# Folds split into halves and spread over a window's steps, row loads issued a window later

## The chip, the cores and the metric

The kernel runs on one NeuronCore of a Trainium2 chip. The metric is the device time of one launch in microseconds, taken as the median of several runs. PE (TensorE), DVE (VectorE), ACT (ScalarE) and POOL (GpSimd) each run their own instructions in the order in which the program lists them, and wait for one another by semaphores; SP (SyncE) and POOL issue the DMAs.

## What is computed

```python
def _attn_ref(x):                       # x: 8 x 3008 x 256
    X = np.fft.fft(x, axis=1)
    X = np.fft.fft(X, axis=2)
    return X.real.astype(np.float32)

def _moe_ref(x, w_in, w_out):           # x: 24064 x 256, w_in: 256 x 2048, w_out: 2048 x 256
    h = np.maximum(x @ w_in, 0.0)
    return (h * h @ w_out).astype(np.float32)
```

The real part of a two-dimensional Fourier transform mixes each of the 8 sequences over its 3008 positions and its 256 features. A feed-forward layer follows, with a squared relu between its two products. Inputs reach the kernel as float32 and are worked on in half precision on the chip; the output is float32.

## The kernel before

**Symmetry.** A real Fourier transform of row k and of row 3008 - k share their products. The kernel computes a cosine part `zc` and a sine part `zs` for half the rows only. A step's sum of both gives one half of the output rows, and turning the sign of the sine part gives the mirrored half. Before the matmuls each sequence is *folded*: rows are added to or subtracted from their mirror images, over features and positions, which shrinks what has to be multiplied.

**Units, blocks, windows.** The eight sequences are taken in the order i = 0 to 7 (`bs` puts sequence 0 last, so i = 7 is sequence 0, and i = 6 is the last sequence in memory, `b + 1 == B`). Each gives two units, odd rows (i, 0) and even rows (i, 1), laid behind one another as columns. The columns are cut into 25 windows, of 512 columns from window 6 on. A window w has eight steps s0 to s7 (`NST`). In each step PE does the first feed-forward product for 256 of the 2048 hidden features of this window (lines 804 to 831), and an eighth of the second product of the window before (`part`, L679). In between it computes z for units that a later window needs (`z_steps`, L567).

**Two kinds of steps.** In a plain step, `pq` (L808, L809) forms the sum, ACT takes its relu (L840), `turn` (L831) changes the sine's sign in PSUM, and ACT takes the relu of the mirrored half. A step listed in `diff[w]` goes another way: `cosines` (L817), then on DVE `twice` (L821) forms t = n - 2 cos, `sines` (L826) adds the sine part, ACT takes one relu and DVE the other (`TENSOR_ADD_SAT`, L838) with the help of t. The rows n are made on POOL: `spread_nyq` brings one row of `zs` to all partitions (PE, then ACT as `zn`, L761), and `nyq_rows` multiplies it (L769), two instructions a step, into three buffers of the pool `wp`. Where step 0 is in the next window's list, the first two of these stand at s5 and the others at s6 of the window before; else at s6 and s7. There are two PSUM buffers for the sums (`ps_h`), so step s + 2 can't start before both relus of step s are done. Squares are DVE's (`power`, L847), which `settle` lets run a step later, or ACT's (`power_act`, L851).

**Loading and folding a sequence.** `load_x` fills a tile of four quarters: two direct quarters and two whose rows come in reverse order by an indirect DMA (`gather`, L132). Two sequences need a row by itself. For sequence 7 (i = 6) the index of the third quarter differs (`idx_c`) and row 1 of that quarter comes by a small DMA (L150); for sequence 0 (i = 7) one row of the first quarter does (L143). Each of them overwrites what a gather has put there, and waits for that gather.

`fold_steps(i)` returns the jobs of one sequence, all but the DMAs on DVE:
- `d_even`: copy a row (L417), add features to their mirror into `fe` (L418, 3072 elements a partition), copy column 0 of all quarters (L419)
- `n_cos` (L429), `d_odd` (L422, 3072 elements), `n_sin` (L432), `odds` (L435, what the odd unit needs), `nyq` (two tiny PE matmuls and a copy, L440 to L442)
- `even` (L447), and in the same job the store of its result to `scr` in DRAM (L449); `back` reads it from there in another order (L457, L459), for the even unit
- `late`: `fold8(0)`, `fold8(1)` (L473), `fold16(0)`, and `fold16(1)` (L484) with `nyq8` (L490 to L492, four copies)
- `load`: `load_x` of the next sequence

**Where the jobs stand.** For i from 2 on, a list is written out by hand: `at_of[w][s]` holds the jobs run in step s of window w behind that step's first relu, `post_of` those behind its share of the second product. With b0 = 5, 8, 10, 13, 16, 19 for i = 2 to 7, `d_even` stands in window b0 - 1 at s1 (at s5 for i = 2 and i = 4), `n_cos` two steps behind it, `d_odd` at s0 of b0, `n_sin` and `odds` at s1, `even` at s3, `nyq` behind s3, `back` at s6, `load` at s7; the late folds in b0 + 1 at s3, s3, s5, s7. For i = 4 window b0 - 1 = 9 is also that of the late folds of i = 3. The order in these lists is the order of each engine's queue.

## Time and profile before

| | |
|---|---|
| median of 3 runs | 631.01 us (630.08 to 633.45) |
| the profiled execution | 630.0 us, span of its instructions 628.0 us |
| mean granted TensorE clock | 0.994 |
| PE busy | 592.7 us (94%) |
| DVE busy | 484.2 us (77%) |
| ACT busy | 460.7 us (73%) |
| POOL busy | 338.9 us (54%) |
| DMA | 47.50 MB, mean 76 GB/s |

A line of the timeline view reads: start and length in us, engine, line of the kernel, operation, what is written and read, how many instructions are merged, and in brackets the idle time of the engine before it with what ended it. A line of the waits view reads: the waiting instruction, what released it, then us in total, times, and the longest. In the windows view the columns are the busy us of each engine, the granted clock, and DMA. "Idle" in brackets is counted from the end of the instruction before, which for PE is a modelled one.

### The profile page before, as it was taken

The numbers are of one execution on the slowest core, as the hardware profiler recorded it, in microseconds if no ns is written. First come the engines' busy times: TensorE is split into PE (matmuls) and PEld (weight loads), VectorE is DVE, ScalarE is ACT, GpSimd is POOL, SyncE is SP. The second block draws the span as 40 slices with busy tenths as digits, with TensorE's granted clock in tenths as the row PEclk, the third lists the DMA queues.
The fourth block names the chain that finished last, engine by engine and source line by source line (L and its number), as shares of the span: only waits on it lengthen the run. The fifth ranks groups of instructions, "written<-read, shape, count | busy, mean of one in ns | idle before, by whom it ended". The sixth has DMA issues, their size and how long they took to land.

```text
span 628.0 us, 11263 instructions
## 1 busy us (share of the span) xinstructions
PE 592.7 (94%) x4441; PEld 427.6 (68%) x4441; DVE 484.2 (77%) x607; ACT 460.7 (73%) x624; POOL 338.9 (54%) x248
## 2 busy tenths in 40 slices
PE   4889999999999999999899979999799999999997
PEld 2457786676666776776677746777467776777786
DVE  7787666978888679878887868878588788777760
ACT  6687777878777776877687856878468787787762
POOL 8220225268808617498086673865838558538520
PEclk9999999999999999999999989999899999999999
DMA  8945321124511461236113431132511311111112
GB/s 150 141 89 131 111 69 33 46 81 84 119 41 43 111 137 43 73 78 133 45 36 106 101 74 49 38 108 66 104 33 50 103 47 49 47 39 44 52 55 67
DMA packets 36523, 47.50 MB, mean 76 GB/s; under 512 B 4215, under 2 KB 30327, under 8 KB 36471
## 3 DMA queue, kind: packets, MB, share of 16 engines
q0 software_dynamic: 9344, 22.14, 17.7%
q1 hardware_dynamic: 26899, 24.44, 13.1%
q8 instruction: 34, 0.56, 0.4%
q10 hardware_dynamic: 228, 0.21, 0.1%
q14 instruction: 18, 0.15, 0.1%
HBM read 33.63 MB, written 27.84 MB: 98 GB/s over the span
## 4 chain that ended last, share of the span: by engine, by line
PE 65%; DVE 13%; POOL 9%; DMA 6%; issue 4%; ACT 3%; POOLq 0%; DVEq 0%
PE po L679 37%; PE ph L831 5%; PE ph L808 5%; PE ph L809 5%; POOL n L769 5%; PE ph L826 5%; PE ph L817 3%; PE pz L567 3%; DVE t L821 3%; DVE h L847 3%; DVE h L838 3%; ACT h L840 2%; DMA xo<-in_x_dram,idx_c 2%; DMA xo<-in_x_dram,idx_f 2%; DMA xo<-in_x_dram,idx_r 1%
## 5 line engine op out<-in xcount | busy, mean ns | idle before, releaser
L840 ACT ACTIVATE h<-ph 128x1024 f16<-128x1024 f32 (+3 forms) x311 | 295.6, 990 | 102.2 <-PE ph L826 82.7
L679 PE MATMUL po<-wout,h 128*128 128x256 f16 (+1 forms) x3024 | 362.8, 273 | 0.0
L769 POOL TENSOR_SCALAR n<-zn,g2n 128x512 f32<-128x512 f16 (+2 forms) x146 | 264.8, 1829 | 165.8 <-ACT zn L761 165.5
L679 PEld LDWEIGHTS <-h 128*128 128x128 f16 (+1 forms) x3024 | 297.2, 99 | 73.1 <-issue 1.3
L847 DVE TENSOR_TENSOR h<-h 128x1024 f16<-128x1024 f16 (+6 forms) x216 | 193.8, 908 | 33.4 <-ACT h L840 30.7
L838 DVE CUSTOM_DVE_ANT_0 h<-t,ph 128x1024 f16<-128x1024 f32 x67 | 81.8, 1221 | 47.7 <-ACT h L840 47.3
L821 DVE SCALAR_TENSOR_TENSOR t<-ph,n 128x1024 f32<-128x1024 f32 (+2 forms) x73 | 87.6, 1200 | 29.7 <-PE ph L817 22.3
L808 PE MATMUL ph<-zc,gh 128*128 128x512 f16 (+3 forms) x238 | 88.4, 372 | 0.4 <-ACT h L900 0.3
L809 PE MATMUL ph<-zs,gh 128*128 128x512 f16 (+3 forms) x238 | 88.4, 372 | 0.0
L851 ACT ACTIVATE h<-h 128x1024 f16<-128x1024 f16 (+2 forms) x73 | 76.1, 1043 | 0.0
L831 PE MATMUL ph<-zs,gh 128*128 128x512 f16 (+3 forms) x238 | 68.1, 368 | 0.0
L694 ACT ACTIVATE osb<-po 128x512 f32<-128x512 f32 (+3 forms) x95 | 55.2, 585 | 11.4 <-PE po L679 10.0
L826 PE MATMUL ph<-zs,gh 128*128 128x512 f16 (+2 forms) x146 | 43.6, 380 | 17.0 <-DVE t L821 16.9
L817 PE MATMUL ph<-zc,gh 128*128 128x512 f16 (+2 forms) x146 | 42.8, 375 | 0.0
L809 PEld LDWEIGHTS <-gh 128*128 128x128 f16 x238 | 23.4, 98 | 26.4 <-issue 1.9
L808 PEld LDWEIGHTS <-gh 128*128 128x128 f16 x238 | 23.4, 98 | 25.7 <-issue 1.1
L826 PEld LDWEIGHTS <-gh 128*128 128x128 f16 x146 | 13.8, 97 | 22.6 <-issue 19.4
L572 ACT ACTIVATE es<-pz 128x376 f32<-128x376 f32 (+1 forms) x32 | 15.5, 487 | 17.5 <-PE pz L567 17.4
L831 PEld LDWEIGHTS <-gh 128*128 128x128 f16 x238 | 22.1, 98 | 5.4
L817 PEld LDWEIGHTS <-gh 128*128 128x128 f16 x146 | 14.3, 98 | 16.7
L459 POOL DMA_INDIRECT rb<-scr,idx_r x16 | 20.6, 1288 | 4.9 <-issue 4.9
L132 POOL DMA_INDIRECT xo<-in_x_dram,idx_r x15 | 18.3, 1219 | 4.5 <-issue 4.0
(142 smaller groups left out, 355.3 us busy)
## 6 DMA issues: line engine op xcount, KB each, us to landing
out_dram<-osb SPq DMA_DIRECT2D x77, 128.0 KB
xo<-in_x_dram POOLq DMA_DIRECT2D x7, 768.0 KB
scr<-ev POOLq DMA_DIRECT2D x8, 390.0 KB, 2.8
rb<-scr POOLq DMA_DIRECT2D x16, 130.0 KB
out_dram<-osb SPq DMA_DIRECT2D x12, 94.0 KB
w<-in_moe_w_in_dram POOLq DMA_DIRECT2D x2, 512.0 KB, 11.2
wout<-in_moe_w_out_dram POOLq DMA_DIRECT2D x1, 1024.0 KB
out_dram<-osb SPq DMA_DIRECT2D x8, 75.0 KB
```

The lines of the kernel that those rows point to most:

```text
L679: nc.tensor.matmul(po[0:m, j * D : (j + 1) * D], h2[:, fc, q : q + m], wout16[:, fc, :], start=(fc == 0), stop=(fc == NFC - 1))
L769: nc.gpsimd.tensor_scalar(out=n2[:, a, 0:wn1], in0=zns[wt][:, 0:wn1], scalar1=g2n[:, fc : fc + 1], scalar2=None, op0=ALU.mult)
L808: nc.tensor.matmul(ph[:, a, 0:wn], gh[:, 0, f0 : f0 + P], zcw[:, 0:wn], start=True, stop=False)
L809: nc.tensor.matmul(ph[:, a, 0:wn], gh[:, 1, f0 : f0 + P], zsw[:, 0:wn], start=False, stop=True)
L817: nc.tensor.matmul(ph[:, a, 0:wn], gh[:, 0, f0 : f0 + P], zcw[:, 0:wn], start=True, stop=True)
L821: nc.vector.scalar_tensor_tensor(out=t2[:, :, 0:wn], in0=phs[s][:, :, 0:wn], scalar=-2.0, in1=n2s[w, s][:, :, 0:wn], op0=ALU.mult, op1=ALU ...
L826: nc.tensor.matmul(phs[s][:, a, 0:wn], gh[:, 1, f0 : f0 + P], zsw[:, 0:wn], start=False, stop=True, skip_group_check=True)
L831: nc.tensor.matmul(phs[s][:, a, 0:wn], gh[:, 2, f0 : f0 + P], zsw[:, 0:wn], start=False, stop=True, skip_group_check=True)
L838: nc.vector._custom_dve(TENSOR_ADD_SAT, out=h, in0=t2s[s][:, :, 0:wn], in1=phs[s][:, :, 0:wn], s0=BIG, s1=0.0)
L840: nc.scalar.activation(h, phs[s][:, :, 0:wn], AF.Relu, bias=0.0, scale=-1.0)
L847: nc.vector.tensor_tensor(h, h, h, op=ALU.mult)
L851: nc.scalar.activation(h, h, AF.Square, bias=0.0, scale=1.0)
```

## The change

Seven things change together.

1. `load_x` no longer issues the two small row loads. They move to `load_rows(i)`, which is put at s7 of window b0 - 2 of that sequence, a window after the gathers.
2. `d_even` and `d_odd` can do half of the quarters at a time (0 and 1, or 2 and 3). The first half of `d_even` also does both copies, for i > 1 on ACT.
3. `d_even`'s halves stand two steps apart (s1, s3; for i = 2 at s5, s7; for i = 4 at s5, s6), `n_cos` behind them (s5; s0 of b0 for i = 2; s7 for i = 4).
4. In b0 the halves of `d_odd` stand at s0 and s1, `n_sin` at s2, `odds` at s5 and `nyq` behind s6.
5. The store to `scr` becomes a job of its own, `away`, at s4.
6. `nyq8` does two copies in place of four, and is a job of its own; the five late jobs stand at s3 to s7 of b0 + 1.
7. `diff` of window 9 becomes (0, 2) in place of (2, 6), so the rows n for its s0 are made in window 8.

```diff
         gather(2, idx["r" if b + 1 < B else "c"][:, 0:1], o + (S - R * (P - 1)) * D)
+        gather(3, idx["r"][:, 0:1], o + (H - R * (P - 1)) * D)
+        return t
+
+    def load_rows(i):
+
+        b, t = bs[i], xs[i]
+        o = b * S * D
+        if b == 0:
+            nc.gpsimd.dma_start(out=t[0:1, 0, R - 1, :], in_=bass.AP(tensor=x.tensor, offset=x.offset + o, ap=[[D, 1], [1, D]]))
         if b + 1 == B:
             nc.gpsimd.dma_start(
                 out=t[1:2, 2, :, :].rearrange("p c d -> p (c d)"),
                 in_=bass.AP(tensor=x.tensor, offset=x.offset + o + (S - R) * D, ap=[[XW, 1], [1, XW]]))
-        gather(3, idx["r"][:, 0:1], o + (H - R * (P - 1)) * D)
-        return t
...
-        def d_even():
-            nc.vector.tensor_copy(t[0:1, 2, 0, :], t[0:1, 0, R - 1, :])
-            nc.vector.tensor_tensor(fef[:, :, 1:129], lo, hi, op=ALU.add)
-            nc.vector.tensor_copy(fef[:, :, 0:1], xf[:, :, 0:1])
-
-        def d_odd():
-            nc.vector.tensor_tensor(fof[:, :, 1:129], lo, hi, op=ALU.subtract)
+        def d_even(h=None):
+            a, z = (0, 4 * R) if h is None else (2 * R * h, 2 * R * (h + 1))
+            if a == 0:
+                for o, v in ((t[0:1, 2, 0, :], t[0:1, 0, R - 1, :]), (fef[:, :, 0:1], xf[:, :, 0:1])):
+                    if i > 1:
+                        nc.scalar.activation(o, v, AF.Copy, bias=0.0, scale=1.0)
+                    else:
+                        nc.vector.tensor_copy(o, v)
+            nc.vector.tensor_tensor(fef[:, a:z, 1:129], lo[:, a:z], hi[:, a:z], op=ALU.add)
+
+        def d_odd(h=None):
+            a, z = (0, 4 * R) if h is None else (2 * R * h, 2 * R * (h + 1))
+            nc.vector.tensor_tensor(fof[:, a:z, 1:129], lo[:, a:z], hi[:, a:z], op=ALU.subtract)
...
+
+        def away():
             scr = drp.tile([R * P, 260], F16, name="scr", tag="scr")
...
-            for slot in range(2):
-                nc.vector.tensor_copy(xt[:, 0, slot, :, 130:131], rev_dim(xt[:, 1, 1 - slot, :, 128:129], 1))
-            nc.vector.tensor_copy(spn[:, 0, :, 0:1], yt[:, 1, 0, :, 128:129])
-            nc.vector.tensor_copy(spn[:, 1, :, 0:1], yt[:, 0, 0, :, 128:129])
-
-        late = [lambda: fold8(0), lambda: fold8(1), lambda: fold16(0), lambda: (fold16(1), nyq8())]
+            nc.vector.tensor_copy(xt[:, 0, :, :, 130:131], rev_dim(rev_dim(xt[:, 1, :, :, 128:129], 1), 2))
+            nc.vector.tensor_copy(spn[:, :, :, 0:1], rev_dim(yt[:, :, 0, :, 128:129], 1))
+
+        late = [lambda: fold8(0), lambda: fold8(1), lambda: fold16(0), lambda: fold16(1), nyq8]
...
     for i in range(2, B):
         b0 = (win_of(col_of[i, 0]) + win_of(col_of[i - 1, 1])) // 2 - 1
-        both = i > 2 and len(at_of[b0 - 1][3]) > 0
-        at_of[b0 - 1][0 if i > 2 else 5].append(lambda i=i: make(i))
-        put(at_of, b0 - 1, 5 if i == 2 or both else 1, i, "d_even")
-        put(at_of, b0 - 1, 7 if i == 2 or both else 3, i, "n_cos")
-        for s, name in ((0, "d_odd"), (1, "n_sin"), (1, "odds"), (3, "even"), (6, "back"), (7, "load")):
-            put(at_of, b0, s, i, name)
-        put(post_of, b0, 3, i, "nyq")
+        tight = b0 - 2 in [(win_of(col_of[j, 0]) + win_of(col_of[j - 1, 1])) // 2 - 1 for j in range(2, i)]
+        near = i == 2 or tight
+        at_of[b0 - 1][0].append(lambda i=i: make(i))
+        at_of[b0 - 2][7].append(lambda i=i: load_rows(i))
+        put(b0 - 1, 5 if near else 1, i, "d_even", 0)
+        put(b0 - 1, (6 if tight else 7) if near else 3, i, "d_even", 1)
+        put(b0 if i == 2 else b0 - 1, 0 if i == 2 else 7 if near else 5, i, "n_cos")
+        put(b0, 0, i, "d_odd", 0)
+        put(b0, 1, i, "d_odd", 1)
+        put(b0, 2, i, "n_sin")
+        put(b0, 3, i, "even")
+        put(b0, 4, i, "away")
+        put(b0, 5, i, "odds")
+        put(b0, 6, i, "back")
+        put(b0, 6, i, "nyq", d=post_of)
+        put(b0, 7, i, "load")
+        for k, s in enumerate((3, 4, 5, 6, 7)):
+            late(b0 + 1, s, i, k)
         if b0 > 5:
             diff[b0] = (2, 4, 6)
-        for st in range(4):
-            at_of[b0 + 1][(3, 3, 5, 7)[st]].append(lambda i=i, st=st: folds[i]["late"][st]())
-        if both:
-            diff[b0 - 1] = (2, 6)
+        if tight:
+            diff[b0 - 1] = (0, 2)
```

The sequences i = 0 and i = 1, which windows 1 to 4 fold, keep whole folds and copies on DVE; only `away`, the order of the copies in `d_even` and the five late jobs reach them.

More of the change, by code (lines that the diff above doesn't have):

```diff
@@ L142, in load_x @@
             gather(0, idx["f"][:, 0:1], o + D)
-            nc.gpsimd.dma_start(out=t[0:1, 0, R - 1, :], in_=bass.AP(tensor=x.tensor, offset=x.offset + o, ap=[[D, 1], [1, D]]))
             direct(1, 2)
@@ L488, in nyq8 @@
             xt, yt = st["xt"], st["yt"]
-            for slot in range(2):
-                nc.vector.tensor_copy(xt[:, 0, slot, :, 130:131], rev_dim(xt[:, 1, 1 - slot, :, 128:129], 1))
-            nc.vector.tensor_copy(spn[:, 0, :, 0:1], yt[:, 1, 0, :, 128:129])
-            nc.vector.tensor_copy(spn[:, 1, :, 0:1], yt[:, 0, 0, :, 128:129])
-        late = [lambda: fold8(0), lambda: fold8(1), lambda: fold16(0), lambda: (fold16(1), nyq8())]
-        return {"u_odd": u_odd, "u_part": u_part, "v_even": v_even, "v_part": v_part, "d_even": d_even, "n_cos": n_cos, "odds": odds, "d_odd": d_odd, "load": load, "n_sin": n_sin, "nyq": nyq, "even": even, "back": back, "late": late}
+            nc.vector.tensor_copy(xt[:, 0, :, :, 130:131], rev_dim(rev_dim(xt[:, 1, :, :, 128:129], 1), 2))
+            nc.vector.tensor_copy(spn[:, :, :, 0:1], rev_dim(yt[:, :, 0, :, 128:129], 1))
+        late = [lambda: fold8(0), lambda: fold8(1), lambda: fold16(0), lambda: fold16(1), nyq8]
+        return {"u_odd": u_odd, "u_part": u_part, "v_even": v_even, "v_part": v_part, "d_even": d_even, "n_cos": n_cos, "odds": odds, "d_odd": d_odd, "load": load, "n_sin": n_sin, "nyq": nyq, "even": even, "away": away, "back": back, "late": late}
     gh = const.tile([P, 3, F], F16, name="gh")
@@ L714, in fold_jobs @@
         f = folds[i] = fold_steps(i)
-        return [f["d_even"], f["n_cos"], lambda: (f["d_odd"](), f["load"]()), f["n_sin"], f["odds"], f["nyq"], f["even"], f["back"]]
+        return [f["d_even"], f["n_cos"], lambda: (f["d_odd"](), f["load"]()), f["n_sin"], f["odds"], f["nyq"], lambda: (f["even"](), f["away"]()), f["back"]]
     NST = NFC // 2
@@ L720, with put, late @@
     diff = {w: (0, 2, 4, 6) if w > 5 else (4, 6) for w in range(4, NW)}
-    def put(d, w, s, i, name):
-        d[w][s].append(lambda: folds[i][name]())
+    def put(w, s, i, name, *k, d=at_of):
+        d[w][s].append(lambda: folds[i][name](*k))
+    def late(w, s, i, *st):
+        at_of[w][s].append(lambda: run(*[folds[i]["late"][k] for k in st]))
     def make(i):
@@ L784 @@
             te = table_steps(1)
-            at = [[folds[1]["even"]], [lambda: te["freq"](), lambda: te["args"](0)], [lambda: f0s["v_part"](0)], [lambda: f0s["v_part"](1), f0s["even"], f0s["back"]],
+            at = [[folds[1]["even"], folds[1]["away"]], [lambda: te["freq"](), lambda: te["args"](0)], [lambda: f0s["v_part"](0)], [lambda: f0s["v_part"](1), f0s["even"], f0s["away"], f0s["back"]],
                   [lambda: te["turns"](0)], [lambda: te["mods"](0)], [lambda: te["absm"](0), lambda: te["sins"](0)], [lambda: te["coss"](0)]]
@@ L788 @@
             at[0] = [lambda: te["weigh"]()]
-            for st in range(4):
-                at[1 + st // 2] = at[1 + st // 2] + f0s["late"][st : st + 1]
+            for st in range(5):
+                at[1 + st // 3] = at[1 + st // 3] + f0s["late"][st : st + 1]
             at[3] = [folds[1]["back"]]
@@ L793 @@
         elif w == win_of(col_of[1, 1]) - 1:
-            for st in range(4):
-                at[st] += folds[1]["late"][st : st + 1]
+            for st in range(5):
+                at[min(st, 3)] += folds[1]["late"][st : st + 1]
             lo, hi = 4, NST - 1
```

## The prediction

> **What bounds the kernel now.** First the page: TensorE is busy 94% of a span of 628.0 us, so only the time in which it stands still can be won. Then the table of waits, which names what it stands for:

> ```profile
> PE ph L826 <- DVE t L821: 16.9, 13, 4.5
> ...
> POOL xo L150 <- DMA xo<-in_x_dram,idx_c: 9.6, 1, 9.6
> ...
> POOL xo L143 <- DMA xo<-in_x_dram,idx_f: 8.9, 1, 8.9
> ...
> DVE t L821 <- POOL n L769: 7.1, 2, 4.1
> ```

> The columns are us in total, times, longest. Once the start is over, almost every stop of PE is one kind: `sines` (L826) waits for `twice` (L821) on DVE, 13 times. Twice that goes back to POOL, whose rows L769 stood behind two small loads that waited for a gather to land. I call windows w, their steps s0 to s7, and T the start of a window's first cosines. Window 15, POOL, then PE:

> ```profile
> 354.29 1.01 POOL L132 DMA_INDIRECT xo<-in_x_dram,idx_c  x1 [0.30 <-issue]
> 364.94 0.57 POOL L150 DMA_DIRECT2D xo<-in_x_dram  x1 [9.64 <-DMA xo<-in_x_dram,idx_c]
> ...
> 366.86 14.69 POOL L769 TENSOR_SCALAR n<-zn,g2n 128x512 f32<-128x512 f16 x8
> ```

> ```profile
> 365.61 1.91 PE L679 MATMUL po<-wout,h 128*128 128x256 f16 x16
> 371.32 1.01 PE L826 MATMUL ph<-zs,gh 128*128 128x512 f16 x2 [3.79 <-DVE t L821]
> 372.12 0.63 PE L808 MATMUL ph<-zc,gh 128*128 128x512 f16 x1
> 372.55 0.63 PE L809 MATMUL ph<-zs,gh 128*128 128x512 f16 x1
> ```

> Sixteen such matmuls start 1.75 apart in all, so L826 could have started at 367.36 and lost 3.96 (by starts; the bracket counts from a modelled end, some 0.17 less). Then matmuls start 0.43 apart where 0.22 is usual: the clock is halved for some 2.5 us (0.79 over 368 to 376), 1.26 more. Window 18 has 4.64 and 1.26 likewise (450.23).

> The other stops are big folds ahead of `twice` on DVE. Window 12 (T = 290.16):

> ```profile
> 290.84 0.42 DVE L484 TENSOR_TENSOR xy<-xy 128x520 f16<-128x520 f16 x1
> 291.18 0.65 DVE L490 COPY xy<-xy 128x2 f16<-128x2 f16 x2
> ...
> 291.88 1.21 DVE L821 SCALAR_TENSOR_TENSOR t<-ph,n 128x1024 f32<-128x1024 f32 x1
> ...
> 296.83 0.48 DVE L417 COPY xo<-xo 1x256 f16<-1x256 f16 x1
> 297.35 2.19 DVE L418 TENSOR_TENSOR fe<-xo 128x3072 f16<-128x3072 f16 x1
> 299.46 0.20 DVE L419 COPY fe<-xo 128x24 f16<-128x24 f16 x1
> 299.55 1.21 DVE L821 SCALAR_TENSOR_TENSOR t<-ph,n 128x1024 f32<-128x1024 f32 x1
> ```

> ```profile
> 297.05 1.91 PE L679 MATMUL po<-wout,h 128*128 128x256 f16 x16
> 300.81 0.59 PE L826 MATMUL ph<-zs,gh 128*128 128x512 f16 x2 [1.85 <-DVE t L821]
> ```

> Here 297.05 + 1.75 = 298.80 against 300.81: 2.0 lost. By the same reading the stops before L826 are: w4 1.24 (and 0.26 behind it), w6 0.24, w7 0.70 and 1.64, w8 0.71, w9 0.50, w10 0.81, w12 0.81 and 2.02, w15 3.96 and 0.49, w18 4.64 and 0.74, w21 0.81; with 2 x 1.26 of slow clock, 22.1 us. This is the pot.

> **The change, part by part.**

> *Last fold of s7 moved to s6, four nyquist copies made two.* At s7 DVE had fold16 and four copies (290.84 to 291.88, 1.04) ahead of `twice`. What stays is a copy of four columns and one of spn; single copies took 0.32 and 0.16, so some 0.4. Fold16 now stands in s6, where DVE waits 0.81 for ACT anyway. `twice` starts 0.65 earlier, and the stops at s0 (0.70, 0.81, 0.81 in w7, w12, w21) fall to 0.05, 0.15, 0.15. Gain 2.0; bounds 1.2 (copies as dear as before) to 2.3 (nothing left).

> *d_even in halves, its two copies on ACT.* The 297 to 299.55 stretch is 2.7 of DVE. Left at s1 is one half: 2.19 / 2 = 1.1, or 1.79 / 2 = 0.9 as the same fold took where POOL was idle (w9). So `twice` comes 1.6 earlier: w12 2.02 to 0.35, w7 1.64 to 0.05 (PE has z work until 172.8 there), w4 1.24 + 0.26 to 0.1. The second half meets `twice` of s4 with 1.1 where n_cos of 0.96 stood and lost 0.05: nothing. n_cos goes to s5. Gain 4.7; bounds 2.7 (each half 0.5 dearer, with 0.5 in each second place) and 5.2. The copies on ACT are not in the trace: 128x6 took 0.23 there (L400), 128x256 0.39; I take 0.35 and 0.25. ACT sat idle 3.38 before its next relu in w12, which covers them; uncovered they cost 0.6 in six windows, 3.6.

> [...]

> *d_odd in halves at s0 and s1, n_sin at s2, odds at s5, its nyquist step at s6.* Before, w8 had n_sin 0.96 and odds 1.26 between the power at 194.25 and `twice` at 197.66; now a half d_odd of 0.9 stands there. The stops of 0.71 and 0.81 (w8, w10) go; three of 0.13 in w13, w16, w19 also. At s5 odds of 1.2 is less than the 2.5 that d_even put there in w4. Its nyquist matmuls come at s6, a step after odds, so PE need not wait for them. Store at s4 in a job of its own: POOL's wait of 2.3 for DVE before it moves, and nobody waits for POOL there. Gain 1.9; bounds 1.2 and 2.0.

> *Late folds one a step* (w6 0.24 to 0.1): 0.15.

> *Window 9 (i = 4, tight).* d_even was at s5, 0.50 lost; diff (2, 6) becomes (0, 2), the same number. But the rows for its s0 are now due in w8 and stand in POOL's queue ahead of the four scr reads: two rows 3.4, reads 4.4, two rows 3.4, starting 4.8 before T (as in w12, 285.42 against 290.16). So x's load goes out at T + 6.5 instead of T + 1.9, and its last gather, which landed at 230.44 = T + 16.3, at T + 20.9. ACT meets its fe copy in s5 near T + 18.3 and stands 2.6; behind it are relu (1.0) and osb, and PE's s7 (T + 22.5) finds its PSUM at T + 23.1. I take 0.6: this window breaks even (-0.1). Bounds: 0 and 3 (a gather of 12 us as measured, and 2 more).

> *The small loads.* They leave the queue between the gathers: rows for w15 and w18 begin when zn is there (360.3 and 438.6, T - 4.8), as in w12, and the stops of 3.96, 0.49, 4.64, 0.74 and 2.52 of clock go: 12.35. But `load_rows` is put at s7 of window b0 - 2, behind **all eight rows** of the next window. In w12 these took

> ```profile
> 285.42 13.36 POOL L769 TENSOR_SCALAR n<-zn,g2n 128x512 f32<-128x512 f16 x8 [3.10 <-ACT zn L761]
> ```

> until T + 8.6. The sixteen completions of L150's load came 1.65 after its issue began (366.6 against 364.94), of L143's 1.7. So it lands at T + 10.3. Who needs it? In w15 the fe copy on ACT (it reads column 0 of all quarters, row 1 of quarter 2 among them); in w18 the xo copy on ACT and the first half on DVE (they read row 0 that the load brings). All are at s1. In w12 ACT's square ends at 296.55, T + 6.4, less 0.65 gained at s0: T + 5.75. ACT is in order, so behind it wait osb (0.5) and relu of s1 (1.0), which frees the PSUM for s3.
> - w15: fe copy done T + 10.55, relu done T + 12.1. PE began s3 at 301.24 in w12, 2.3 of stops included that now go: 301.24 - 290.16 - 2.3 = T + 8.8. **3.3 lost.**
> - w18: DVE's half ends T + 11.4, `twice` T + 12.6; PE would be ready at 298.80 - 290.16 - 0.65 = T + 8.0. **4.6 lost**, and like 3.96 and 4.64 long enough for the slow clock, 1.2.
> With the remnants of s0 and s2 (0.5 and 0.15) 9.75 are given back of 12.35: gain 2.6. Bounds: rows at 14.69 for eight as in w15, 1.3 later in each window, and slow clock in w15: -1.3; no loss at all if ACT and DVE reached the load later: 11.7.

> [...]

> **Sum.** 2.0 + 4.7 + 1.9 + 0.15 - 0.1 + 2.6 = 11.2. The profiled execution took 630.0 (span 628.0 and 2.0 around it), the median of the runs is 631.01; against that, 619.8. All bounds at their worst (1.2 + 2.7 + 1.2 - 2.5 - 1.3, and ACT's copies half uncovered, 1.8, = -0.5) are 631.5; at their best (2.3 + 5.2 + 2.0 + 0.3 + 0.5 + 11.7 = 22.0) 609.

> **Rivals.**
> 1. *The small loads are harmless*: both stops vanish whole. For it: the load itself takes 1.65. Against: POOL's order, eight rows at 1.67 each, and copies at s1. 619.8 - 9.1 = 610.7. Chance 0.12.
> 2. *The new waits eat more*: rows at the slow pace and slow clock in both (3.9), w9's load late by 3 (2.4): 626. For it: 14.69 in w15, and ACT's six new in-order waits on loads. Chance 0.18, somewhat under half of it within 0.5% of before.
> 3. *Slower than before*: the same in-order wait in w15 and w18, with the small load later still. Every us of it is a us of PE in both windows, so the gain is gone when it lands 5.6 later, at T + 16; at T + 18 the time is 635. For it: four pairs of rows share three buffers, so the last pair hangs on `twice` of s0, itself on DVE. Against: in w12 the eight ran without a break. Chance 0.08.
> 4. *Halves don't shorten the way to `twice`*: a half that meets one of POOL's rows waits out its 1.6, in w7 and w12, and the halves of d_odd give nothing in w8 and w10 (1.5): 619.8 + 4.7 = 624.5. For it: the fold took 2.19 beside POOL's rows, 1.79 without. Against: that is 0.4, a quarter of a row. Chance 0.10.

> **From these.** The forecast has 0.52, its own range 617 to 623. Between 610 and 627 lie it, rivals 1 and 4 and half of 2, 0.83. Change under 0.5% (3.2 us) can't be told from none by a measurement of this kernel: faster 0.84 (0.52 + 0.12 + 0.10 and 0.10 of rival 2), same 0.08 (the rest of rival 2), slower 0.08 (rival 3).

> **What would show it.** In the profile after: L769 in w15 and w18 starts at zn with no gather ahead; the small load's issue near T + 8.6; ACT's new fe and xo copies released by a DMA, some 4 us each in those two windows and in w9; PE's stop at s3 of w15 (before L808, released by ACT) and before L826 at s2 of w18; L826's stops elsewhere under 0.4. If ACT shows no wait for a load, rival 1 holds; if the halves run over 1.3 each, rival 4.

## The result, and the profile after

The changed kernel takes 624.62 us, the median of four runs (624.06 to 627.89), beside 631.65 for the kernel before in the same comparison (four runs). The ratio is 0.9888, 95% interval 0.984 to 0.9935: 7.0 us less, where 11.2 were forecast. The profiled execution is the slowest of the four (627.9, span 626.1). A second profile of the same kernel, taken later, has a span of 623.4; where the two differ matters below.

To put numbers on where PE stands still, I add up, step by step, by how much the starts of successive matmuls lie further apart than their usual spacing (0.22 for 512 columns, 0.11 for 256). A window without any stop then shows about 0.45, which is the zero of this table: with the spacing read to a thousandth (0.216 and 0.109) it shows 0.00 to 0.02.

| stretch (window and step) | before | after | again |
|---|---|---|---|
| start (window 1) | 2.4 | 5.8 | 5.1 |
| w7, w12, w21: s0 | 2.5 | 1.6 | 1.6 |
| w4: s6, s7; w7, w12: s2 | 5.4 | 1.3 | 1.3 |
| w8, w10, whole windows | 2.6 | 1.4 | 1.4 |
| w9 | 1.0 | 0.5 | 0.5 |
| w15 | 6.5 | 7.6 | 6.1 |
| w18 | 7.2 | 7.8 | 7.3 |

The folds did what they were to do; windows 15 and 18 gave nothing. The waits view of the kernel after shows what stands in them now (us in total, times, longest):

```profile
PE ph L849 <- DVE t L844: 6.8, 10, 4.3
...
ACT fe L426 <- DMA xo<-in_x_dram: 4.5, 1, 4.5
ACT xo L426 <- DMA xo<-in_x_dram: 4.5, 1, 4.5
DVE fe L429 <- DMA xo<-in_x_dram: 4.0, 1, 4.0
PE ph L831 <- ACT h L863: 3.4, 1, 3.4
```

`sines` (now L849) waits 6.8 instead of 16.9, and POOL's waits of 9.6 and 8.9 for a gather are gone. In their place ACT waits for the small load itself, once in each window, and DVE once. Window 15 (T = 362.24) in the timeline of the kernel after, POOL, ACT, then PE:

```profile
357.50 13.67 POOL L792 TENSOR_SCALAR n<-zn,g2n 128x512 f32<-128x512 f16 x8 [3.37 <-ACT zn L784]
371.12 0.61 POOL L157 DMA_DIRECT2D xo<-in_x_dram  x1
```

```profile
368.30 0.40 ACT L426 ACTIVATE xo<-xo 1x256 f16<-1x256 f16 x1
373.21 0.31 ACT L426 ACTIVATE fe<-xo 128x24 f16<-128x24 f16 x1 [4.51 <-DMA xo<-in_x_dram]
373.37 0.60 ACT L705 ACTIVATE osb<-po 128x512 f32<-128x512 f32 x1
373.86 1.93 ACT L863 ACTIVATE h<-ph 128x1024 f16<-128x1024 f32 x2
```

```profile
370.92 0.59 PE L849 MATMUL ph<-zs,gh 128*128 128x512 f16 x2 [0.21 <-DVE t L844]
374.93 0.58 PE L831 MATMUL ph<-zc,gh 128*128 128x512 f16 x1 [3.42 <-ACT h L863]
375.31 0.63 PE L832 MATMUL ph<-zs,gh 128*128 128x512 f16 x1
375.74 0.63 PE L831 MATMUL ph<-zc,gh 128*128 128x512 f16 x1
376.17 0.63 PE L832 MATMUL ph<-zs,gh 128*128 128x512 f16 x1
376.59 3.62 PE L690 MATMUL po<-wout,h 128*128 128x256 f16 x16
```

Read it downwards: eight rows keep POOL until 371.12; only then is the load of one row issued; it lands at 373.1; ACT, in order, stands at its copy from 368.7, and behind that copy are the output copy and the relu that frees PSUM for L831. PE could have gone on at 370.92 + 0.43 = 371.35 and starts at 374.93: 3.58 lost. Then the starts lie 0.43 apart, and sixteen matmuls that take 1.75 take 3.4: the granted clock is 0.50 from 373.70 to 380.52. Window 18 shows the same through DVE (its half of the fold waits 4.02 for the load, `twice` behind it):

```profile
448.04 1.91 PE L690 MATMUL po<-wout,h 128*128 128x256 f16 x16
454.27 1.01 PE L849 MATMUL ph<-zs,gh 128*128 128x512 f16 x2 [4.32 <-DVE t L844]
```

454.27 - 449.79 = 4.48. What the folds gained is seen in window 12 (T = 289.26), DVE and PE:

```profile
290.10 0.16 DVE L502 COPY xy<-xy 128x4 f16<-128x4 f16 x1
290.17 0.59 DVE L503 COPY spn<-xy 128x4 f16<-128x4 f16 x1
290.66 1.21 DVE L844 SCALAR_TENSOR_TENSOR t<-ph,n 128x1024 f32<-128x1024 f32 x1
...
295.81 0.96 DVE L429 TENSOR_TENSOR fe<-xo 128x1536 f16<-128x1536 f16 x1
296.69 1.21 DVE L844 SCALAR_TENSOR_TENSOR t<-ph,n 128x1024 f32<-128x1024 f32 x1
```

```profile
291.92 0.59 PE L849 MATMUL ph<-zs,gh 128*128 128x512 f16 x2 [0.32 <-DVE t L844]
...
297.95 0.59 PE L849 MATMUL ph<-zs,gh 128*128 128x512 f16 x2 [0.21 <-DVE t L844]
```

One half of 0.96 stands ahead of `twice` where 2.7 stood, and the stop of 2.0 is 0.38 (297.95 against 295.82 + 1.75). At s0 the copies are two instead of four, but the second takes 0.59 instead of the 0.16 of the first, and 0.48 is lost where 0.15 was forecast.

### The profile page after: what moved, and what is told of

Its sections match the earlier page's. It is cut to its first block, busy times and chain, and to the rows that moved or that the text cites. A ratio compares the mean times of both kernels' runs of the same rounds, so it can differ in the third digit from the quotient of the medians.

```text
span 626.1 us, 11275 instructions
## 1 busy us (share of the span) xinstructions
PE 596.9 (95%) x4441; PEld 429.4 (69%) x4441; DVE 481.7 (77%) x591; ACT 464.1 (74%) x636; POOL 337.4 (54%) x248
## 4 chain that ended last, share of the span: by engine, by line
PE 80%; DVE 8%; POOL 6%; DMA 2%; ACT 2%; issue 2%; POOLq 0%; DVEq 0%; ACTq 0%
PE po L690 46%; PE ph L831 7%; PE ph L832 7%; PE ph L854 7%; PE ph L849 5%; PE ph L840 4%; POOL n L792 4%; PE pz L578 4%; DVE h L870 2%; DVE t L844 2%; DMA xo<-in_x_dram,idx_r 2%; DVE h L861 1%; ACT h L863 1%; PE pn L783 1%; DMA xo<-in_x_dram 1%
## 5 line engine op out<-in xcount | busy, mean ns | idle before, releaser
L870 DVE TENSOR_TENSOR h<-h 128x1024 f16<-128x1024 f16 (+6 forms) x216 | 197.4, 924 | 42.4 <-ACT h L863 39.9
L831 PE MATMUL ph<-zc,gh 128*128 128x512 f16 (+3 forms) x238 | 89.4, 376 | 3.8 <-ACT h L863 3.4
L849 PE MATMUL ph<-zs,gh 128*128 128x512 f16 (+2 forms) x146 | 43.2, 377 | 6.8 <-DVE t L844 6.8
L831 PEld LDWEIGHTS <-gh 128*128 128x128 f16 x238 | 23.6, 99 | 26.0 <-issue 1.6
L840 PEld LDWEIGHTS <-gh 128*128 128x128 f16 x146 | 14.3, 98 | 16.9 <-issue 0.3
L132 POOL DMA_INDIRECT xo<-in_x_dram,idx_r x15 | 18.7, 1248 | 4.5 <-issue 4.3
L849 PEld LDWEIGHTS <-gh 128*128 128x128 f16 x146 | 13.2, 97 | 11.5 <-issue 8.5
```

What stands on the lines that cost most here:

```text
L831: nc.tensor.matmul(ph[:, a, 0:wn], gh[:, 0, f0 : f0 + P], zcw[:, 0:wn], start=True, stop=False)
L840: nc.tensor.matmul(ph[:, a, 0:wn], gh[:, 0, f0 : f0 + P], zcw[:, 0:wn], start=True, stop=True)
L849: nc.tensor.matmul(phs[s][:, a, 0:wn], gh[:, 1, f0 : f0 + P], zsw[:, 0:wn], start=False, stop=True, skip_group_check=True)
L870: nc.vector.tensor_tensor(h, h, h, op=ALU.mult)
```

## The experiments

Theory A: the halves and moved jobs gained some 7 to 8, and the small loads, moved behind all eight rows, gave back what they gained, through an in-order wait of ACT and DVE. Rival B: the move of the loads is good, and what is missing went elsewhere. All ratios are against the kernel before, with 95% intervals.

### The load move undone, and alone

`rows_back` is the changed kernel with the small loads between the gathers again:

```diff
-        at_of[b0 - 2][7].append(lambda i=i: load_rows(i))
```
(and the two `dma_start` back in `load_x`.)

> The changed kernel with the small loads back between the gathers, as before; halves, spreading and ACT's copies stay. Theory A (moving the loads as the change does it is worth next to nothing: one stop was traded for another): windows 15 and 18 lose 4 to 5 at s0 with slow clock as before, none at s2 and s3, and the time is that of the changed kernel within 2: 623 to 627. Rival B (the move is what made the kernel faster): 630 or more.

623.61 us, ratio 0.9878 (0.9842 to 0.9915), against 0.9888 (0.984 to 0.9935) with the move. Windows 15 and 18 lose 7.2 and 7.4, at s0 and s1, much as before. So the move is worth nothing that these intervals can tell from zero: B falls.

`only_rows_s7` is the kernel before with that move alone.

> The kernel before with the move of the small loads alone (to s7 of window b0 - 2); folds whole and on DVE. Theory A: in windows 15 and 18 DVE meets its fold at T + 6.4, waits for the load until T + 10.3, folds for 2.7 and only then comes to twice, which ends at T + 14.2; PE is ready at T + 8.6, so 5.6 are lost in each and 2.5 of slow clock, 0.8 at s0 besides, against 5.7 and 6.6 before: slower than before, about 637. Rival B (taking the loads out of the queue between the gathers is a gain by itself): 620 to 626.

635.30 us, ratio 1.0093 (1.006 to 1.0125): slower. With the undivided fold and its copies on DVE behind the late load, for which DVE waits 3.4 and 6.1, windows 15 and 18 lose 8.8 and 10.8. This is rival 3's mechanism (the in-order wait), and it decides where nothing else is changed.

### The load one step earlier

`rows_s6` issues the small load after two of the eight rows:

```diff
-        at_of[b0 - 2][7].append(lambda i=i: load_rows(i))
+        at_of[b0 - 2][7 if tight else 6].append(lambda i=i: load_rows(i))
```

> The changed kernel with the two small loads one step earlier (s6 in place of s7 of window b0 - 2), so that POOL issues them behind two rows n of the next window in place of all eight. Theory A (the stops of windows 15 and 18 come only from the load standing behind eight rows): the load lands near T + 2, ACT and DVE reach it at T + 5.8, both stops (3.6 and 4.5) and the slow clock behind them (2.7 and 2.4) vanish, no POOL row comes late: about 612. Rival B (ACT's in-order copies wait for the gathers anyway, or POOL then waits for the gather and the rows come late): the stops only change their name, 622 to 626.

616.91 us, ratio 0.9793 (0.9764 to 0.9823), 7.7 less than the changed kernel by one step. No wait of ACT or DVE for the load is left. But both windows lose 2.00 at s0 instead of the usual 0.53, which A had not foreseen. DVE and POOL there in the timeline of `rows_s6`:

```profile
360.35 2.46 DVE L870 TENSOR_TENSOR h<-h 128x1024 f16<-128x1024 f16 x2
362.74 0.44 DVE L502 COPY xy<-xy 128x4 f16<-128x4 f16 x1
362.81 1.91 DVE L503 COPY spn<-xy 128x4 f16<-128x4 f16 x1
363.75 1.21 DVE L844 SCALAR_TENSOR_TENSOR t<-ph,n 128x1024 f32<-128x1024 f32 x1
```

```profile
359.93 0.61 POOL L157 DMA_DIRECT2D xo<-in_x_dram  x1
360.57 5.21 POOL L792 TENSOR_SCALAR n<-zn,g2n 128x512 f32<-128x512 f16 x3
```

Two products that take 1.44 in the kernel after take 2.46, and a copy of four columns 1.91. `twice` starts about 1.5 later than it would. 

`only_rows_s6` is the kernel before with the loads moved to the same place.

> The kernel before with the two small loads alone moved, to s6 of window b0 - 2, behind two rows n. Theory A: no wait for the load is left and no row comes late, so windows 15 and 18 lose what window 12 loses before (0.8 at s0, 2.0 at s2, about 3.3 in all with the steps' own) in place of 6.5 and 7.2: about 7 less, 624.5. Rival B (the load waits for the gather on POOL again and holds the rows): 628 to 632.

624.98 us, ratio 0.992 (0.9894 to 0.9946). The time is what A said, and no wait for the load is left, but the windows don't lose as A said: they lose 4.4 and 4.1, not the 3.3 of window 12. At s0 they lose 2.2 and 1.7 instead of the 0.85 that they lose in `only_rows_s7`. These two kernels differ in nothing but the step of the load, so it is the load at this place, between the rows, that costs this, as in `rows_s6`. Between step 7 and step 6, the same one line decides 10 us of the kernel before (635.3 against 625.0) and 8 of the changed one.

### The readers moved, not the load

`fold_s3` leaves the load behind the rows and moves what reads it:

```diff
-        put(b0 - 1, 5 if near else 1, i, "d_even", 0)
-        put(b0 - 1, (6 if tight else 7) if near else 3, i, "d_even", 1)
-        put(b0 if i == 2 else b0 - 1, 0 if i == 2 else 7 if near else 5, i, "n_cos")
+        put(b0 - 1, 5 if near else 3, i, "d_even", 0)
+        put(b0 - 1, (6 if tight else 7) if near else 5, i, "d_even", 1)
+        put(b0 if i == 2 else b0 - 1, 0 if i == 2 else 7, i, "n_cos")
```

> The changed kernel, its small loads left at step 7 (behind the eight rows), but the halves of d_even at steps 3 and 5 instead of 1 and 3 and n_cos at step 7 instead of 5: not the load but its readers are moved, about 5.5 us later, behind the landing at T + 10.3. Theory A (the stops of windows 15 and 18 are the in-order wait of ACT and DVE for the small load): both stops and the slow clock behind them go, the two windows lose 1.4 each as window 12 does instead of 7.6 and 7.8, and as nothing is issued on POOL ahead of the rows, DVE is not held at step 0 either: 624.6 - 12.5 = 612, up to 614 if n_cos at step 7 costs 0.4 in four windows. Rival B (these windows lose for another reason, POOL's rows or the slow clock by itself): 623 to 625.

613.3 us, ratio 0.9714 (0.9687 to 0.974). Window 15 loses 1.0 instead of 7.6, window 18 1.7 instead of 7.8; the granted clock is 1.00 from 368 to 384 and from 432 to 456. With the load untouched, the stop is gone: it was the wait for the load. A holds.

### Halves, copies, nyquist

`whole` is `rows_s6` with both folds undivided, each at its first half's place:

```diff
-        put(b0 - 1, 5 if near else 1, i, "d_even", 0)
-        put(b0 - 1, (6 if tight else 7) if near else 3, i, "d_even", 1)
+        put(b0 - 1, 5 if near else 1, i, "d_even")
...
-        put(b0, 0, i, "d_odd", 0)
-        put(b0, 1, i, "d_odd", 1)
+        put(b0, 0, i, "d_odd")
```

> The changed kernel with the small loads at step 6 (616.9), and d_even and d_odd undivided, each where its first half stood; the copies stay on ACT. Theory A (the halves shorten the way to twice): the undivided d_even is 1.0 longer ahead of twice: about 1.0 lost again in window 7, 1.4 in window 12, as much in 15 and 18 where it isn't hidden by the hold at step 0, 0.7 in window 4: 4 to 6 more, 621 to 623. d_odd undivided at step 0 costs nothing, since before lost nothing there. Rival (the copies on ACT and the moved jobs did it, not the halves): 617 to 618.

`copies_dve` is `rows_s6` with the fold's two copies on DVE (`if i > B` in place of `if i > 1`).

> The changed kernel with the small loads at step 6 (616.9), and the two copies of d_even back on DVE ahead of the first half. Theory A: they are 0.48 and 0.20 there, about 0.5 lost in each of windows 4, 7, 12, 15 and 18: 2 to 2.5 more, 619. Rival: on ACT they delay the relu as much as they delay twice on DVE, and the time stays at 617, or falls.

`whole` takes 620.67 us, ratio 0.9832 (0.98 to 0.9864), 3.8 more than `rows_s6`; `copies_dve` 620.38, ratio 0.983 (0.9799 to 0.9862), 3.5 more, where 4 to 6 and 2 to 2.5 were expected. The intervals just touch that of `rows_s6`, so the windows decide. Window 12 of each, DVE:

```profile
297.69 1.77 DVE L429 TENSOR_TENSOR fe<-xo 128x3072 f16<-128x3072 f16 x1
299.39 1.21 DVE L842 SCALAR_TENSOR_TENSOR t<-ph,n 128x1024 f32<-128x1024 f32 x1
```

```profile
296.57 0.48 DVE L428 COPY xo<-xo 1x256 f16<-1x256 f16 x1
297.08 0.63 DVE L428 COPY fe<-xo 128x24 f16<-128x24 f16 x1
297.59 0.96 DVE L429 TENSOR_TENSOR fe<-xo 128x1536 f16<-128x1536 f16 x1
298.47 1.21 DVE L844 SCALAR_TENSOR_TENSOR t<-ph,n 128x1024 f32<-128x1024 f32 x1
```

The undivided fold puts 0.8 more ahead of `twice`, the copies 1.0, and PE loses 0.8 and 1.0 more at s2 (1.23 and 1.45 against 0.42). Both parts are worth about the same, and each is felt one for one. The halves of d_odd are another matter: undivided at s0 it costs nothing in window 8 (the whole window loses 0.54 against 0.87), so what came from there in the change came from the jobs that were moved (n_sin, odds and what hangs on them), not from the halves.

`fold_s3_nyq` is `fold_s3` with the nyquist copies at step 6:

```diff
-        for k, s in enumerate((3, 4, 5, 6, 7)):
+        for k, s in enumerate((3, 4, 5, 6, 6)):
```

> The kernel with the readers moved to steps 3 and 5, and besides the nyquist copies at step 6 behind the last fold instead of at step 7. Theory A: they are the 0.5 still lost at step 0 in five windows (0.59 each beside a row of POOL), and at step 6 DVE has time for them: 1.6 less than the kernel with the readers moved alone, some 610.5. Rival: two copies more ahead of the next twice put the stop a step earlier, and the time is the same as with the readers moved alone.

610.33 us, ratio 0.9687 (0.9659 to 0.9715); s0 loses 0.06 in windows 7, 12, 15, 18 and 21 instead of 0.53, which is 2.3. So the copies were what was left there. One stop remains that it didn't touch: in window 18 the load landed at 442.5, when its readers had asked at 440.9, and PE lost 1.67 at s4.

### Three ways to end it

`rows_s5` is the changed kernel with the loads at step 5, ahead of all rows (`7 if tight else 5`); `best_s5` is the same edit on `fold_s3_nyq`.

> The changed kernel with the small loads at step 5 of window b0 - 2, ahead of all rows, instead of step 6, between the second and the third. At step 6 they landed in time, but step 0 of windows 15 and 18 lost 2.0 each instead of the usual 0.5, with DVE stretched (2.46 for two folds that take 1.44) from the moment POOL issues the load. Theory H (issuing a load in software on POOL holds DVE, and the place of the issue decides what it costs): at step 5 the hold falls on work with 0.8 of slack before relu, so step 0 loses 0.5 again in both windows: 616.9 - 3.0 = 614, or 615 if a part of the hold shows at step 6. Rival (it is the splitting of the rows or the load's own data that costs, not the place): 616 to 618.

> The kernel with the readers moved to steps 3 and 5 and the nyquist copies at step 6 (610.3), and besides the small loads at step 5 of window b0 - 2. In window 18 the load still landed 1.6 after its readers asked (442.56 against 440.9), and PE lost 1.67. Theory A: that stop goes, 1.2 to 1.6 less, 609. If the issue holds DVE at a place without slack (theory H), up to 1.5 is given back in each of two windows: 609 to 612.

615.37 us (ratio 0.9749, 0.9711 to 0.9788) and 612.48 (0.9698, 0.9668 to 0.9728): the first is 1.5 less than step 6, which the intervals don't separate, the second is no better than the 610.33 without the edit. The place of the load isn't all that counts here. From the waits view of `rows_s5`:

```profile
POOL xo L157 <- DMA xo<-in_x_dram,idx_c: 6.6, 1, 6.6
...
POOL xo L155 <- DVE xy L497: 4.8, 1, 4.8
```

At step 5 the gather has not landed, so POOL stands in its queue for it again, and the rows start late: the wait that the change removed is back in small. (The second line names DVE, which had long been done; in `best_s5` the same wait is put down to the gather of idx_f, 4.4.) In `rows_s5` `twice` waits 0.8 in each window for its rows. Theory H, that issuing the load is what held DVE in `rows_s6`, isn't settled by this run: DVE takes 1.51 for the pair in window 15, the usual time, but 0.66 for one copy in both windows.

`fold_s4_nyq` moves the readers by one more step instead:

```diff
-        put(b0 - 1, 5 if near else 3, i, "d_even", 0)
-        put(b0 - 1, (6 if tight else 7) if near else 5, i, "d_even", 1)
+        put(b0 - 1, 5 if near else 4, i, "d_even", 0)
+        put(b0 - 1, (6 if tight else 7) if near else 6, i, "d_even", 1)
```

> The kernel of 610.3 with the halves of d_even at steps 4 and 6 instead of 3 and 5, the small loads left behind the rows at step 7. Theory A (what decides is only whether the readers come after the landing): the 1.67 of window 18 goes without touching the loads, 609. Rival: at the even steps the half and then n_cos at step 7 stand ahead of another twice, 0.4 in four windows, and the time is 610 to 611.

608.27 us (607.58 to 610.59), ratio 0.965 (0.9619 to 0.968): the lowest of all, 16 less than the changed kernel; from the 610.33 of `fold_s3_nyq` its interval doesn't separate it, but the stop of window 18 is gone. From its waits view:

```profile
PE ph L849 <- DVE t L844: 0.5, 2, 0.3
...
ACT xo L426 <- DMA xo<-in_x_dram: 0.2, 1, 0.2
```

Windows 12, 15 and 18 each lose 0.42, as a window without any big fold does. The second line says how near it is: in window 18 ACT still asks 0.2 before the load lands.

### The changed kernel a second time

> The changed kernel itself, a second profiled execution. If the start is chance (the landing of the third gather, 35.3 to 37.8 in ten profiles with the same issue times), window 1 loses something else than 5.80, anywhere between 1.9 and 6.8, while windows 15 and 18 lose their 3.6 and 4.5 again; the length of the half clock behind these, 5.3 in the first profile, is read here a second time: theory says at least 2.5, and if 5.3 was chance it is another.

625.18 us in one run, span 623.4. The start lost 5.1, windows 15 and 18 6.1 and 7.3. The stops themselves repeat (3.43 and 4.85 against 3.58 and 4.48), the clock behind them does not. The windows view of the first profile, then of the second (the column after POOL's is the granted clock):

```profile
368.00:376.00 8.00, 4.37 (x26) 2.48 (x25) 3.95 (x4) 3.29 (x6) 3.73 (x3) 0.86 0.11 33
376.00:384.00 8.00, 8.00 (x44) 5.08 (x43) 5.20 (x6) 4.08 (x5) 0.00 (x0) 0.72 0.11 29
```

```profile
368.00:376.00 8.00, 4.53 (x26) 2.51 (x24) 4.11 (x5) 2.61 (x6) 3.03 (x3) 0.85 0.11 33
376.00:384.00 8.00, 8.00 (x60) 5.96 (x59) 5.95 (x7) 6.15 (x7) 0.00 (x0) 0.94 0.13 36
```

From 376 on 60 matmuls ran in eight us against 44. The half clock cost 2.7 and 2.3 behind the two stops in the first profile, 1.4 and 1.5 in the second. In finer windows the granted clock is 0.50 from 373.70 to 380.52 and from 452.20 to 459.03 in the first, 6.8 us each. In the second the granted 0.85 and 0.94 above make 3.4 us of half clock behind the first stop, and 0.79 over 448 to 456, with 1.00 over 456 to 464, as much behind the other.

## Why the prediction was right in direction and too high in size

**The new wait: right.** Forecast were rows from zn (T - 4.8) to T + 8.6, the load at T + 10.3, ACT at its copy at T + 5.75, and 3.3 and 4.6 lost. In window 15 the rows run from T - 4.7 to T + 8.9, the load lands at T + 10.9, ACT finishes its first copy and stands from T + 6.5, and 3.58 and 4.48 are lost. `fold_s3` shows the cause: move the readers behind the landing and the stops go, with the load where it was. Rival 1 (loads harmless) falls with the ACT waits. Of rival 2 the slow clock in both windows came; its slow rows (eight took 13.67 and 13.24) and its late load in window 9 did not, and the time lies between the forecast and its 626. Rival 3 came true only where the other parts of the change are missing (`only_rows_s7`).

**The slow clock behind it: mis-sized, by more than any other term of the sum.** The prediction gave window 18 1.2 and window 15 nothing, with a slow clock there only among the bounds; it took 2.5 us of half clock from the kernel before as its length. That was read too short already: the granted clock there is 0.50 from 371.16 to 374.57 and from 449.66 to 453.08, 3.4 us each, and by the starts of the matmuls it cost 1.58 and 1.38. After the change it cost 5.0 in the one profile and 2.9 in the other. So the small loads gave -1.7 and +0.3 (windows 15 and 18 together, 13.7 before against 15.4 and 13.4), not +2.6. `rows_back` says the same with times: the move is worth nothing. In the kernel before and in the kernel after, no half clock between the first 30 us and the last matmul is shorter than 3.41 us. The 3.4 us ahead of 371.16 and of 449.66 held no matmul in the kernel before, but in those ahead of 373.70 and of 452.20 in the kernel after PE was busy for 1.0 and 1.2. No run shows the 2.5 that the 1.2 of window 18 came from: the three profiles of the two kernels show 3.4 or 6.8 us of half clock behind these stops.

**Nyquist and fold16 at s0: mis-sized.** Forecast 2.0, measured 0.9 (0.2, 0.3 and 0.3 in windows 7, 12 and 21, rounded). I took 0.4 for two copies from rows where single ones took 0.16 to 0.32, but beside the rows of POOL one of the two takes 0.58 to 0.59. `fold_s3_nyq` moves them to a step where DVE has time, and gets what was missing.

**Halves of d_even and the copies: right.** Forecast 4.7, measured 4.1 in windows 4, 7 and 12, with halves of 0.96 and copies of 0.40 and 0.31 (forecast 0.9 to 1.1, 0.35 and 0.25). `whole` and `copies_dve` show both parts. Rival 4 (a half waits out a row of 1.6) falls, no run shows such a wait: in the kernel after no half of d_even took over 0.97, and of the twelve halves of d_odd two took 1.33 and 1.37.

**d_odd: right sum, partly the wrong reason.** Forecast 1.9, measured 1.6, but `whole` shows that the halves had no share in it.

**Window 9: forecast -0.1, measured +0.5.** The load went out at T + 6.5 as forecast, but its last gather landed 9.0 after its issue, at T + 17.9, where 12 and T + 20.9 were reckoned. So ACT met no late load there; the 2.6 of waiting didn't come.

**The start: not in the prediction.** Window 1 lost 2.4 in the profile before and 5.8 and 5.1 in those after. In ten profiles POOL issues the last two gathers at the same times (25.98 to 26.09 and 27.34 to 27.45), and the last one's first reader starts anywhere from 35.3 to 37.8. From the timelines of the kernel after and of `fold_s4_nyq`, which share this code:

```profile
37.58 1.78 DVE L429 TENSOR_TENSOR fe<-xo 128x3072 f16<-128x3072 f16 x1
```

```profile
35.43 1.78 DVE L429 TENSOR_TENSOR fe<-xo 128x3072 f16<-128x3072 f16 x1
```

So the fold that waits for the landing starts 2.15 apart in two executions of the same code. The changed order of the copies there has no visible share: where the first reader starts at 35.75 in the kernel before, window 2 begins at 53.57; where it starts at 35.77 in `fold_s3_nyq`, which has the changed start, at 53.58. What cost more in the two profiles after is the later landing, and the half clock behind that stop. Whether the change makes late landings likelier isn't shown: three traces have the old start, eleven the new.

In sum, for the profiled pair: 0.9 + 4.1 + 1.6 + 0.5 - 0.1 (late folds) - 1.7 - 3.4 (start) = 1.9, the difference of the spans 628.0 and 626.1; for the second profile 0.9 + 4.1 + 1.6 + 0.5 - 0.1 + 0.3 - 2.7 = 4.6, of 628.0 and 623.4. The medians lie 7.0 apart. That both profiles after drew a dear start, and that the profiled execution before was faster than its median (630.0 against 631.65), fits this, but runs without a trace can't show it.

## What to carry to other kernels

When an instruction moves out of a queue, ask at the new place what stands ahead of it and what reads its result, and put the readers behind the landing with a step to spare: here one line, a step earlier or later, decided 8 to 10 us, and moving the readers did at least as well as moving the load (613.3 against 616.9 at step 6 and 615.4 at step 5, of which the intervals separate only the first). A copy that is moved to a less busy engine takes its wait along: here ACT stood 4.5 for each load, and the relu behind its copies came so late that PE stood 3.42. Stops of PE like those here (3.43 to 4.85) are to be priced with their slow clock as a range (here 1.4 to 2.7 for each), not with one length read from one execution, and that length is to be read from the granted clock.

## What the runs showed of the hardware

```profile
47.29 1.04 PE L578 MATMUL pz<-sin,od 128*128 128x376 f16 x3 [2.15 <-DVE od L453]
48.12 1.15 PE L578 MATMUL pz<-cos,od 128*128 128x376 f16 x3
```

```profile
47.48 0.65 PE L572 MATMUL pz<-sin,od 128*128 128x376 f16 x3 [2.15 <-DVE od L447]
47.97 0.64 PE L572 MATMUL pz<-cos,od 128*128 128x376 f16 x3
```

Three matmuls start 0.83 before the next ones in the one, 0.49 in the other.

What tells them apart isn't shown by these two timelines. By the starts, the slow matmuls of `rows_s6` begin at 47.42 and end at 50.84. The 3.41 us ahead of 47.42 held 0.94 us of matmuls at their usual spacing, and the 3.41 us up to the same place in `only_rows_s6` (47.61) 0.85. The kernels before and after show more. Past the first 30 us and up to the last matmul the granted clock is 0.50 for 3.413 us at 371.16 and 449.66 in the kernel before; in the kernel after it is so for 3.413 at 49.43 and for 6.827 at 373.70 and 452.20. The starts lie 78.51 apart in the one and 324.27 and 78.51 in the other, which is 23, 95 and 23 times 3.413. Cut from these starts into stretches of 3.413, the two profiles hold 0, 0, 0.79, 0.70 and 1.00 us of matmuls in the stretches ahead of a half clock, and 1.33 or more in every other one at full clock between 30 and 620. So it may hang on where a stop falls whether it costs a half clock; that is my estimate from these five, and no run moves a stop to try it. What the runs do show is that the same stop of 2.15 was followed by a half clock in one kernel and not in the other, and that stops of 3.4 to 4.9 were followed by 3.4 us of it in one execution of the changed kernel and by 6.8 in another.

A small DVE instruction beside POOL's rows took quite different times. In the kernel after the copy of four columns (L503) took 0.16 to 0.18 where no row ran (85.75) or where it began 1.5 and 1.7 into one (240.62, 109.24), and 0.59 where it began 0.28 into one (363.14). In `rows_s6`, where the load's 0.61 stands on POOL between the rows, it took 1.91. (The next instruction began 0.94 behind its start there, 0.49 in the kernel after.) The two products ahead of it took 2.46 there and 1.44 in the kernel after. In part both sides are longer: where a half of d_even began before a row was through (window 7, at 172.98) the half took its usual 0.96, and the row that started at 173.37 took 1.99, where rows beside none of DVE's TENSOR_TENSOR took 1.55 to 1.59. But no product of those in window 15 of the kernel after waited a row out: one with 1.34 of its row to come took 1.01 (at 364.77), and one that began 1.15 into a row its usual 0.68 (at 362.47). So a pair that took 1.44 in one kernel took 1.0 more in the next. That the load between the rows brings this about is shown by `only_rows_s6` beside `only_rows_s7`, and the pair of products took 2.44 there too; that it does so by shifting the rows is my reading, and no run shows it by itself.
